# Two passes instead of three in the spatial sum, a closing pass over two tiles, a late gelu, and a bias added at the first evacuation

## The chip, the cores and the metric

The kernel runs on one core of one Trainium2 chip. The metric is the device time of one execution of the program, in microseconds (us), on that core. Medians of several executions are given with their range. An execution counts as slow when it is over 1.5% above the fastest of the same kernel; the executions compared here are fast ones. The profile of a kernel is one execution of it; its "span" (first to last instruction) is some 1.5 to 2 us shorter than the time. The profile also gives the clock that TensorE was granted, as a share of full speed.

Engine names in the profile: PE is TensorE's matmuls, PEld its weight loads, DVE is VectorE, ACT is ScalarE, POOL is GpSimd.

## The reference

Two layers, each an attention block and then a mixer over the sequence, both with residuals. S = 2048 rows, D = 512, 32 heads of 16 that share one key and value head, mixer width 1792.

```python
def _A_ref(x, wq, wk, wv, wo):                 # attention
    q = (x @ wq).reshape(B, S, 32, 16) ...
    k = x @ wk; v = x @ wv
    p = softmax(q k^T * 16 ** -0.5)            # 32 x 2048 x 2048 scores
    return (p v) ... @ wo

def _B_ref(x, w_in, w_sp, b_sp, w_out):        # mixer
    z = gelu(x @ w_in)
    z1 = z[..., :896]
    z2 = layernorm(z[..., 896:])
    g = einsum('ts,bsf->btf', w_sp, z2) + b_sp[None, :, None]   # the "spatial" sum over all 2048 rows s
    return (z1 * g) @ w_out

x = x + _A_ref(layernorm(x), ...)
x = x + _B_ref(layernorm(x), ...)
# and both once more
```

## The kernel before

All data is bf16, with f32 sums in PSUM (the memory that the matmuls write to; an instruction that takes a sum out of it is called an evacuation here). The kernel is written as a generator: a Python list scheduler gives every instruction a priority, dependencies and an estimated duration, and lays out the order of all five engines when the kernel is built. The parts that matter here:

- The softmax needs exp of 4096 score blocks of 128x512 (2048 a layer). ScalarE does most of them, in instructions of 3 or 2 blocks; VectorE does the rest with a polynomial, in six lines of instructions for a batch of 3 blocks.
- Rows are finished in groups ("chunks"). When a chunk's attention is done, its part of the mixer up to z2 is computed beside the softmax of the next chunk. A gelu on ScalarE interrupts the exps and costs two table loads, one there and one back.
- The spatial sum needs z2 of all 16 row tiles of 128. Tiles come with the chunks, so the sum is made in passes: each pass multiplies the tiles that are ready and adds the result into an fp16 buffer `gp`. The last tile is done in a closing pass, which also multiplies by z1 and by w_out.
- Two PSUM banks serve all of these side jobs and VectorE's score blocks.
- "Warm-up" matmuls, zero times zero, are put in where TensorE has had little to do in the last 3.41 us, to keep its clock up.

The passes, the batches of gelu by chunk, and the number of tiles left to the closing pass:

```python
        self.chunks = [[256, 256, 512, 512, 256, 128, 128], [512, 512, 512, 256, 128, 128]]
        self.passes = [[(0, 8, 2), (8, 12, 3), (12, 15, 5)], [(0, 8, 1), (8, 12, 2), (12, 15, 4)]]
        self.gelus = [[(0, 1, 2), (3,), (4, 5), (6,)], [(0, 1), (2,), (3, 4), (5,)]]
        self.s_fin = 15
```

The gelu of a batch of chunks, and what follows it:

```python
        # in mixer(), after the matmuls with w_in ...
        if g.ci != batch[-1]:
            return
        T, z1, z2 = [[x for h in self.held for x in h[i]] for i in range(3)]
        zs = [h[3] for h in self.held]
        self.held = []
        t0 = T[0]
        ...
        def gl2(e):
            return e.activation(z2f[:, t0 * FH:(t0 + nt) * FH], z2f[:, t0 * FH:(t0 + nt) * FH], ACTF.Gelu_apprx_tanh)
        if last:
            gs = z2
            pre = sc.op("act", lambda e: e.activation(self.tiny[:], self.mhalf[:], ACTF.Exp), 0.1, z1 + z2, 2.0, table="exp")
        else:
            gs = [sc.op("act", gl2, d_gelu(nt * FH), z1 + z2, -1.0, table="gelu")] * (2 * nt)
            z1 = [sc.op("act", gl1, sum(d_gelu(NF * zn) for _t, zn, _v in zs), z1 + z2, -0.9, table="gelu")]
        ... # z1 goes to DRAM; z2 is normalized tile by tile (bn_stats, bn_aggr, pow, tensor_scalar)
        sc.rush = 0.0
        for (s0, s1, ci) in self.passes[g.layer]:
            if ci == g.ci:
                self.spatial(s0, s1, g.layer)
        if last:
            self.closing(g.layer)
```

One pass of the spatial sum. The bias is a matmul of its own, the `None` in `seq`; the first pass is copied out of PSUM, later passes are added to `gp`:

```python
    def spatial(self, s0, s1, layer):
        sc = self.sc
        acc = s0 > 0
        nst = s1 - s0
        early = s1 == self.s_fin
        pr = 1.6 if early else 2.5 if acc else 4.0
        ... # where the weight slabs of this pass are loaded to
            for f in range(NF):
                seq = ([] if acc else [None]) + list(range(s0, s1))

                def pe(e, b, part, tc=tc, f=f, w_=w_, seq=seq):
                    ins = None
                    for s in part:
                        st, sp = (s == seq[0]), (s == seq[-1])
                        if s is None:
                            ins = e.matmul(self.b32(b), self.ident[:, tc:tc + 1].to_broadcast([P, P]), self.b4[:, :],
                                           start=st, stop=sp)
                        else:
                            ins = e.matmul(self.b32(b), self.z2n[:, s, f * 128:(f + 1) * 128],
                                           w_[:, s - s0, :] if s - s0 < na or not spare else wsp[:, s - s0 - na, :],
                                           start=st, stop=sp)
                    ...
                def ev_fn(e, b, tc=tc, f=f):
                    dst = self.gp[:, tc, f, :]
                    if acc:
                        return e.tensor_tensor(dst, self.b32(b), dst, ALU.add)
                    return e.tensor_copy(dst, self.b32(b))
                pl, (ev,) = sc.job(pieces, [dict(
                    fn=ev_fn, dur=d_psum(512), prio=max(1.0, pr - 1.5),
                    deps=list(self.gp_read[(tc, f)]) + ([self.gp_ops[(tc, f)]] if acc else []))], deps, pr)
```

VectorE takes no score block while a job of the last ("early") pass is ready and has not started:

```python
    def take(self, t, js):

        k = self.k
        sc = k.sc
        if self.hold or sc.bank_free() > t:
            return None
        base = NDB * (self.nb % (NPD // NDB))
        if any(o.start is None and o.ready is not None and o.ready <= t for o in k.early_first):
            return None
        want = sum(o.first and o.prio < URGENT and o.ready <= t for o in sc.ready["pe"])
```

The rule for warm-up matmuls: one is due when the columns multiplied in the last 3.41 us are fewer than the sum in this line, with TICK_COLS = 3060 and WARM = 1600.

```python
        t = sc.below(f, TICK_COLS + WARM + (AHEAD if near else 0.0))   # WarmStream.peek()
```

The softmax here doesn't subtract the row's maximum and nothing guards it: scores larger than these inputs give would overflow.

Of the kernel before, what the change touches and what calls it, by code (L numbers as in the profile page):

```python
# [13 lines left out]
P = 128  # L14
# [6 lines left out]
NF = 7  # L21
# [352 lines left out]
NDB = 3  # L374

# [7 lines left out]
WARM = 1600.0  # L383
# [46 lines left out]
class Kern:  # L430
    def __init__(self, nc, A_x, A_wq, A_wk, A_wv, A_wo, B_x, B_w_in, B_w_sp, B_b_sp, B_w_out, out):
# [10 lines left out]
        self.passes = [[(0, 8, 2), (8, 12, 3), (12, 15, 5)], [(0, 8, 1), (8, 12, 2), (12, 15, 4)]]  # L442
        self.gelus = [[(0, 1, 2), (3,), (4, 5), (6,)], [(0, 1), (2,), (3, 4), (5,)]]
        self.s_fin = 15
# [17 lines left out]
        self.V = sb([P, self.NT, 128], BF16, "V")  # L462
# [5 lines left out]
        self.b4 = sb([P, 512], BF16, "b4")  # L468
# [95 lines left out]
    def load(self, A_x, A_wq, A_wk, A_wv, A_wo, B_b_sp):  # L564
# [24 lines left out]
        zb = sc.op("pool", lambda e: e.memset(self.b4[:], 0.0), 0.5, (), 4.0)  # L589
        self.l_b = self.dma(lambda e: e.dma_start(self.b4[0:4, :], B_b_sp.rearrange("(k t) -> k t", k=4)), [zb], "ldb", 4096)  # L590
# [39 lines left out]
        m = vm(self.V[:], 2048, 0.13)  # L630
        self.z1s_free = [self.c_wk]
        self.c_v = pm(self.V[:].rearrange("p t (c r) -> p t c r", r=32)[:, :, :, DH], 1.0, 64, 0.8, [m])
# [54 lines left out]
    def layer_keys(self, layer):  # L687
        sc = self.sc
        for p in range(8):
            def build(p=p):  # L690
# [28 lines left out]
                def vcp(b):  # L719
                    return (self.V[:, ts[0]:ts[0] + 2, :].rearrange("p t (c r) -> p t c r", r=32)[:, :, :, 0:DH],  # L720
                            self.b32(b)[:, 256:256 + 2 * DH].rearrange("p (t d) -> p t d", t=2)[:, :, None, :].to_broadcast([P, 2, 4, DH]))
# [5 lines left out]
                vc = dict(fn=lambda e, b: e.tensor_copy(*vcp(b)), dur=d_psum(128), prio=pr, deps=[self.c_v] + vd_,  # L727
                          alts=[("act", lambda e, b: e.activation(*vcp(b), ACTF.Copy), d_act(128) + 0.1)])
# [106 lines left out]
    def finish_group(self, g, pv_last):  # L835
        sc = self.sc
        nq = g.n // 128
        sc.rush = RUSH if g.fin <= 1 and g.v == 1 else 0.0
# [120 lines left out]
    def mixer_chunk(self, g):  # L959
# [5 lines left out]
        pr = PR_LAST if last else (PR_SMALL if g.fin <= 2 else 3.0)  # L965
# [32 lines left out]
        if last:  # L998
            z1v = self.z1L
            z1_war = list(self.dx_s.end)  # L1000
        elif g.ci < batch[-1] <= self.passes[g.layer][0][2]:
            z1v = self.gp[:, g.ci].bitcast(BF16)[:, :, 0:n]
            z1_war = [o for f in range(NF) for o in self.gp_read[(g.ci, f)]]
        else:
            z1v = self.z1s[:].rearrange("p (f t) -> p f t", f=NF)
            z1v = z1v[:, :, 256:256 + n] if g.fin == 1 else z1v[:, :, 0:n]
            z1_war = list(self.z1s_free)
# [27 lines left out]
        if g.ci != batch[-1]:  # L1035
            return
        T, z1, z2 = [[x for h in self.held for x in h[i]] for i in range(3)]
# [12 lines left out]
        def gl2(e):  # L1050
            return e.activation(z2f[:, t0 * FH:(t0 + nt) * FH], z2f[:, t0 * FH:(t0 + nt) * FH], ACTF.Gelu_apprx_tanh)
        if last:
            gs = z2
            pre = sc.op("act", lambda e: e.activation(self.tiny[:], self.mhalf[:], ACTF.Exp), 0.1, z1 + z2, 2.0, table="exp")
        else:
            gs = [sc.op("act", gl2, d_gelu(nt * FH), z1 + z2, -1.0, table="gelu")] * (2 * nt)
            z1 = [sc.op("act", gl1, sum(d_gelu(NF * zn) for _t, zn, _v in zs), z1 + z2, -0.9, table="gelu")]
        for ci, (zt, zn, v) in zip(batch, zs):
            sp = self.dma(lambda e, zt=zt, zn=zn, v=v: e.dma_start(self.z1_dv[:, :, zt * 128:zt * 128 + zn], v), z1,
                          f"z1s{g.layer}{zt}", zn * P * NF * 2)  # L1060
            self.z1_spill.append((zt * 128, zt * 128 + zn, sp))
            if last:
                self.z1L_spill = sp
            elif ci < batch[-1] <= self.passes[g.layer][0][2]:
                for f in range(NF):
                    self.gp_read[(ci, f)] = [sp]
            else:
                self.z1s_free = [sp] + (self.z1s_free if g.fin == 1 else [])
        ag = []
# [15 lines left out]
        sc.rush = 0.0  # L1085
        for (s0, s1, ci) in self.passes[g.layer]:
            if ci == g.ci:
                self.spatial(s0, s1, g.layer)
        if last:
            self.closing(g.layer)  # L1090
# [10 lines left out]
    def spatial(self, s0, s1, layer):  # L1101
# [4 lines left out]
        pr = 1.6 if early else 2.5 if acc else 4.0  # L1106
        z2f = self.z2n[:].rearrange("p t f -> p (t f)")
        wsl = self.wsT[:].rearrange("p s t -> p (s t)")
        if early:

            self.wsP = []
            nf = self.NT - s1
            parts = [(0, 2, z2f[:, 2048:5120], (2, 3, 4, 5)), (2, 3, z2f[:, 5120:6656], (5, 6, 7)),
                     (3, 4, wsl[:, 0:1536], None)]
            for (c0, c1, w_, tiles) in parts:
                w_ = w_.rearrange("p (s t) -> p s t", s=nst)
                war = self.last_ws[0] if tiles is None else [o for t in tiles for o in self.z2_read[t]]
                ld = self.dma(lambda e, w_=w_, c0=c0, c1=c1: e.dma_start(w_, self.ws_dv[:, s0:s1, 512 * c0:512 * c1]),
                              war + self.ws_st[s0:s1], f"wsp{c0}", (c1 - c0) * nst * 131072, 1.0)
                for tc in range(c0, c1):  # L1120
                    self.wsP.append((w_[:, :, 512 * (tc - c0):512 * (tc - c0 + 1)], ld, tiles))
            self.held_f = range(0, 3)
# [7 lines left out]
        for tc in range(4):  # L1130
            if early:
                w_, ld, held = self.wsP[tc]
# [14 lines left out]
            for f in range(NF):  # L1147
                seq = ([] if acc else [None]) + list(range(s0, s1))

                def pe(e, b, part, tc=tc, f=f, w_=w_, seq=seq):  # L1150
                    ins = None
                    for s in part:
                        st, sp = (s == seq[0]), (s == seq[-1])
                        if s is None:
                            ins = e.matmul(self.b32(b), self.ident[:, tc:tc + 1].to_broadcast([P, P]), self.b4[:, :],
                                           start=st, stop=sp)
                        else:
                            ins = e.matmul(self.b32(b), self.z2n[:, s, f * 128:(f + 1) * 128],  # L1158
                                           w_[:, s - s0, :] if s - s0 < na or not spare else wsp[:, s - s0 - na, :],
                                           start=st, stop=sp)  # L1160
# [3 lines left out]
                deps = [ld] + ([ld2] if spare else []) + [self.z2_op[s] for s in range(s0, s1)] + [self.c_id]  # L1164
# [3 lines left out]
                def ev_fn(e, b, tc=tc, f=f):  # L1168
                    dst = self.gp[:, tc, f, :]
                    if acc:  # L1170
                        return e.tensor_tensor(dst, self.b32(b), dst, ALU.add)  # L1171
                    return e.tensor_copy(dst, self.b32(b))
# [222 lines left out]
class ExpStream:  # L1395
# [31 lines left out]
    def commit(self, t):  # L1427
# [18 lines left out]
        if not nx or nx[0].unit.grp.layer != blocks[0].unit.grp.layer:  # L1446
            if not self.queue:
                for x, (b, n) in enumerate(k.rings["full"]):
                    for i in range(b, b + n):
                        k.sc.lend(i, [i], k.fill_s.exp_of[x])  # L1450
                k.sc.op("act", lambda e: e.activation(k.tiny[:], k.mhalf[:], ACTF.Gelu_apprx_tanh), 0.1, [o, k.c_mh], -2.0,
                        table="gelu")


class PVStream:
# [53 lines left out]
    def commit(self, t):  # L1509
# [3 lines left out]
        def fn(e):  # L1513
            ins = None
            for b in u.blocks:
                j = b.j
                ins = e.matmul(k.b32(u.grp.pvb)[32 * j:32 * j + 32, :], k.V[:, u.kt, 32 * j:32 * j + 32], b.slot,  # L1517
# [14 lines left out]
class DexStream:  # L1532
# [29 lines left out]
    def take(self, t, js):  # L1562
# [3 lines left out]
        if self.hold or sc.bank_free() > t:  # L1566
            return None
        base = NDB * (self.nb % (NPD // NDB))
        if any(o.start is None and o.ready is not None and o.ready <= t for o in k.early_first):
# [257 lines left out]
```

## Time and profile before

| | before |
|---|---|
| time, median of 3 (range) | 1803.42 us (1802.94 to 1805.38) |
| span of the profile, mean granted clock | 1800.1 us, 0.999 |
| busy: ACT, DVE, PE | 1725.3, 1699.9, 1604.6 us |
| score blocks on ScalarE / VectorE | 3550 / 546 |
| last exp of layer 0, of layer 1, end | 853.8, 1749.1, 1800.1 us |

The head of the profile page of the kernel before: span, busy time of each engine with its share and the number of instructions, and the shares of engines in the chain of work that ended last.

```profile
span 1800.1 us, 29924 instructions
...
PE 1604.6 (89%) x11861; PEld 480.7 (27%) x11949; DVE 1699.9 (94%) x2576; ACT 1725.3 (96%) x1556; POOL 56.2 (3%) x90
...
ACT 45%; DVE 19%; PE 18%; issue 17%; POOL 1%; DMA 0%; ACTq 0%; POOLq 0%; DVEq 0%
```

Three engines are above 89%, so an average does not tell which of them sets the time. The table by windows does. Its rows are stretches of the softmax's end and of the tail of each layer; the columns are named in the first line, with (x) the number of instructions.

```profile
core 0: us, PE busy (x) PEld busy (x) DVE busy (x) ACT busy (x) POOL busy (x), PEclk, DMA share, GB/s
800.00:854.00 54.00, 49.71 (x360) 15.93 (x362) 41.03 (x69) 53.93 (x48) 1.92 (x4) 1.00 0.25 76
854.00:893.00 39.00, 36.07 (x239) 18.98 (x241) 37.78 (x95) 18.44 (x35) 3.63 (x6) 1.00 0.18 50
1640.00:1749.00 109.00, 101.89 (x736) 32.56 (x747) 84.29 (x140) 108.87 (x95) 2.85 (x6) 1.00 0.22 61
...
1763.00:1800.00 37.00, 34.39 (x176) 16.25 (x178) 32.23 (x84) 13.14 (x30) 0.00 (x0) 1.00 0.46 137
```

Until 854 us and until 1749 us ScalarE is busy for 53.93 of 54 and 108.87 of 109 us: in the softmax, time is ScalarE time. In the tail of layer 0 VectorE is the full engine, 37.78 of 39 us, with PE close behind at 36.07. In the last 37 us PE and VectorE have 34.39 and 32.23 us and take turns.

ScalarE's timeline shows the two places where the change acts: a gelu interruption before the end of layer 0, and the closing pass at the end. Columns: start, duration, engine, line, operation, and in brackets the idle time before it with its releaser.

```profile
829.47 1.28 ACT L1051 ACT_TABLE_LOAD   x1
...
835.65 1.28 ACT L1434 ACT_TABLE_LOAD   x1
836.94 16.84 ACT L1434 ACTIVATE Pa<-ps_all 128x1536 bf16<-128x1536 f32 x15
853.80 1.28 ACT L1451 ACT_TABLE_LOAD   x1
...
1749.07 1.28 ACT L1451 ACT_TABLE_LOAD   x1
...
1770.18 0.60 ACT L1229 ACTIVATE E<-ps_all 128x512 f16<-128x512 f32 x1 [3.52 <-PE ps_all L1217]
...
1778.54 0.60 ACT L1229 ACTIVATE E<-ps_all 128x512 f16<-128x512 f32 x1 [4.01 <-PE ps_all L1217]
```

The interruption takes from 829.47 to 836.94, 7.5 us without an exp, 2.56 of them table loads. The closing repeats every 8.36 us (1770.18, 1778.54), two blocks of 256 columns each time.

The groups of VectorE instructions by form (count, then busy us and mean ns, then idle before them) give the price of an evacuation and of a score block:

```profile
L1626 DVE TENSOR_SCALAR E<-ps_all 128x512 f32<-128x512 f32 x546 | 368.7, 681 | 27.1 <-PE ps_all L1774 25.2
...
L1171 DVE TENSOR_TENSOR gp<-ps_all,gp 128x512 f16<-128x512 f32 x112 | 74.5, 684 | 19.4 <-PE ps_all L1158 19.0
...
L1172 DVE CAST gp<-ps_all 128x512 f16<-128x512 f32 x56 | 38.0, 679 | 1.4 <-PE ps_all L1158 1.2
```

There are 168 evacuations of the spatial sum of 0.68 us each. A batch of three score blocks takes 3 x 0.681 for the first line plus five more lines (1.750, 0.950, 0.949, 0.949 and 0.549 us), 2.4 us a block. What ScalarE's exps waited for scores, from the list of waits (total us, times, longest):

```profile
ACT Pa L1434 <- PE ps_all L1774: 11.7, 20, 1.0
```

### The profile page before, as it was taken

How to read it: one execution, taken by the hardware profiler on the slowest of the kernel's cores; microseconds unless marked ns; L12 is line 12 of the kernel's file. 1: busy time of each engine (PE TensorE's matmuls, PEld its weight loads, DVE VectorE, ACT ScalarE, POOL GpSimd, SP SyncE). 2: the span in 40 equal slices, each digit the busy share in tenths (PEclk: the TensorE clock that was granted, in tenths of full speed). 3: DMA queues.
4: the chain of work that ended last, by engine and by line, in shares of the span. 5: the costliest groups of instructions: out<-in, count | busy, mean ns of one | idle time of the engine just before them, and what ended most of it. 6: DMA issues, size and time to landing. Idle time of an engine off the chain costs nothing.

```text
span 1800.1 us, 29924 instructions
## 1 busy us (share of the span) xinstructions
PE 1604.6 (89%) x11861; PEld 480.7 (27%) x11949; DVE 1699.9 (94%) x2576; ACT 1725.3 (96%) x1556; POOL 56.2 (3%) x90
## 2 busy tenths in 40 slices
PE   8888888888989999999998888888889899998999
PEld 4222222222222222223432222222222222222234
DVE  9999999999999999987999999999999889999868
ACT  8999999999999999999589999999999999999993
POOL 2000000000000000000110000000000000000000
PEclk9999999999999999999999999999999999999999
DMA  5444100011011011222120000000111111202223
GB/s 159 100 89 120 58 14 7 7 31 21 16 44 31 27 24 36 60 68 66 53 45 7 7 7 18 18 7 4 30 22 15 45 30 30 50 28 52 64 57 113
DMA packets 155427, 75.64 MB, mean 42 GB/s; under 512 B 108564, under 2 KB 151704, under 8 KB 155288
## 3 DMA queue, kind: packets, MB, share of 16 engines
q1 hardware_dynamic: 153704, 73.56, 15.9%
q8 instruction: 95, 1.56, 0.4%
q10 hardware_dynamic: 1584, 0.16, 0.1%
q14 instruction: 44, 0.36, 0.1%
HBM read 30.97 MB, written 17.83 MB: 27 GB/s over the span
## 4 chain that ended last, share of the span: by engine, by line
ACT 45%; DVE 19%; PE 18%; issue 17%; POOL 1%; DMA 0%; ACTq 0%; POOLq 0%; DVEq 0%
ACT Pa L1434 43%; PE ps_all L1774 5%; PE ps_all L1517 3%; DVE E L1626 3%; PE ps_all L1158 3%; DVE Pd L1657 3%; PE ps_all L1250 2%; PE ps_all L1755 2%; DVE E L1653 1%; DVE E L1655 1%; DVE E L1651 1%; DVE st L641 1%; DVE st L1071 1%; PE ps_all L980 1%; DVE gp L1171 1%
## 5 line engine op out<-in xcount | busy, mean ns | idle before, releaser
L1434 ACT ACTIVATE Pa<-ps_all 128x1536 bf16<-128x1536 f32 (+1 forms) x1425 | 1612.7, 1391 | 13.7 <-PE ps_all L1774 11.7
L1774 PE MATMUL ps_all<-qs,kT 32*128 32x512 bf16 x4096 | 560.1, 385 | 154.1 <-ACT Pa L1434 140.1
L1626 DVE TENSOR_SCALAR E<-ps_all 128x512 f32<-128x512 f32 x546 | 368.7, 681 | 27.1 <-PE ps_all L1774 25.2
L1755 PE MATMUL ps_all<-zero 128*128 128x512 bf16 x1241 | 374.3, 386 | 13.4 <-DVE st L1071 3.7
L1774 PEld LDWEIGHTS ps_all<-qs,kT 32*128 32x128 bf16 x4096 | 138.8, 91 | 728.1 <-ACT Pa L1434 693.5
L1517 PE MATMUL ps_all<-Pa,V 128*32 128x512 bf16 x3550 | 322.1, 385 | 0.9 <-DVE oT L841 0.9
L1657 DVE SCALAR_TENSOR_TENSOR Pd<-E 128x1536 uint16<-128x1536 f32 (+2 forms) x185 | 319.0, 1724 | 2.3
L1158 PE MATMUL ps_all<-wsT,z2n 128*128 128x512 bf16 x668 | 188.4, 382 | 8.7 <-issue 3.9
L1517 PE MATMUL ps_all<-Pd,V 128*32 128x512 bf16 x546 | 187.0, 386 | 0.0
L1655 DVE TENSOR_TENSOR E<-E 128x1536 f16<-128x1536 f16 (+2 forms) x185 | 173.3, 937 | 2.0
L1653 DVE TENSOR_TENSOR E<-E 128x1536 f16<-128x1536 f16 (+2 forms) x185 | 173.2, 936 | 2.0
L1651 DVE TENSOR_SCALAR E<-E 128x1536 f16<-128x1536 uint16 (+2 forms) x185 | 173.1, 936 | 1.4
L1755 PEld LDWEIGHTS ps_all<-zero 128*128 128x128 bf16 x1241 | 92.1, 97 | 203.6 <-issue 145.2
L1654 DVE TENSOR_SCALAR E<-E 128x1536 f16<-128x1536 f16 (+2 forms) x185 | 100.4, 543 | 0.8
L1517 PEld LDWEIGHTS ps_all<-Pa,V 128*32 128x32 bf16 x3550 | 64.7, 94 | 120.9 <-issue 113.6
L1171 DVE TENSOR_TENSOR gp<-ps_all,gp 128x512 f16<-128x512 f32 x112 | 74.5, 684 | 19.4 <-PE ps_all L1158 19.0
L1158 PEld LDWEIGHTS ps_all<-wsT,z2n 128*128 128x128 bf16 x714 | 56.6, 98 | 88.5 <-issue 43.6
L980 PE MATMUL ps_all<-w_in_r,xnTB 128*128 128x448 bf16 x256 | 64.2, 355 | 2.0 <-DVE z2n L991 1.0
L1016 PE MATMUL ps_all<-xnTB,w_in_r 128*128 128x512 bf16 (+2 forms) x364 | 63.0, 299 | 1.1 <-DVE z1s L1027 0.6
L1250 PE MATMUL ps_all<-E 128*128 128x512 bf16 x214 | 52.2, 380 | 4.1 <-DVE E L1235 2.6
L645 POOL TENSOR_SCALAR ve<-mv 128x2 f32<-128x2 f32 (+1 forms) x28 | 11.9, 423 | 1358.4 <-DVE mv L643 1358.3
L841 DVE CAST oT<-ps_all 128x512 bf16<-128x512 f32 x64 | 43.6, 682 | 4.5 <-PE ps_all L1517 4.4
(87 smaller groups left out, 919.0 us busy)
## 6 DMA issues: line engine op xcount, KB each, us to landing
wsT_scratch<-gp SPq DMA_DIRECT2D x16, 512.0 KB, 3.7
wsT<-wsT_scratch SPq DMA_DIRECT2D x8, 1024.0 KB, 5.3
z1s<-z_scratch SPq DMA_DIRECT2D x16, 448.0 KB, 3.7
wsT<-wsT_scratch SPq DMA_DIRECT2D x8, 512.0 KB, 3.5
z_scratch<-z1s SPq DMA_DIRECT2D x4, 896.0 KB, 5.2
X<-in_A_x_dram SPq DMA_DIRECT2D x8, 256.0 KB, 5.5
out_dram<-X SPq DMA_DIRECT2D x16, 128.0 KB, 1.9
w_in_r<-in_B_w_in_dram SPq DMA_DIRECT2D x1, 1792.0 KB, 10.2
```

The source lines that it names most:

```text
L1158: ins = e.matmul(self.b32(b), self.z2n[:, s, f * 128:(f + 1) * 128], w_[:, s - s0, :] if s - s0 < na or not spare else wsp[:, s - s0 - na, :],
L1171: return e.tensor_tensor(dst, self.b32(b), dst, ALU.add)
L1434: return e.activation(k.Pa[:, base:base + n, :], k.b32(b0, n).rearrange("p (k q) -> p k q", k=n), ACTF.Exp, scale=SCALE)
L1517: ins = e.matmul(k.b32(u.grp.pvb)[32 * j:32 * j + 32, :], k.V[:, u.kt, 32 * j:32 * j + 32], b.slot, tile_position=(0, 32 * j), start=u.fir ...
L1626: c = k.sc.op("dve", lambda e: e.tensor_scalar(k.ey[:, s, 512 * i:512 * (i + 1)], k.b32(j.bank.idx)[:, 0:512], E_LOG2, E_BIAS, op0=ALU.mul ...
L1651: o2 = sc.op("dve", lambda e: e.tensor_scalar(x, lo, E_X * 2.0 ** -16, E_X * E_A, op0=ALU.mult, op1=ALU.add), d_sb(n, 0.521e-3), self.ops ...
L1653: o3 = sc.op("dve", lambda e: e.tensor_tensor(w, x, x, ALU.mult), d_sb(n, 0.521e-3), [o2, self.wfree], pr)
L1654: o4 = sc.op("dve", lambda e: e.tensor_scalar(w, w, E_C, None, op0=ALU.add), d_sb(n, 0.26e-3), [o3], pr)
L1655: o5 = sc.op("dve", lambda e: e.tensor_tensor(w, w, x, ALU.mult), d_sb(n, 0.521e-3), [o4], pr)
L1657: o7 = sc.op("dve", lambda e: e.scalar_tensor_tensor(po.bitcast(U16), y, E_D, w, op0=ALU.add, op1=ALU.add), d_sb(n, 1.042e-3), [o5] + self ...
L1755: return e.matmul(k.b32(pvb if b is None else b.idx), k.zero[:], k.zero[:, None, :].to_broadcast([P, 4, P]), start=b is not None, stop=b i ...
L1774: return e.matmul(self.b32(bank), self.kT[32 * j:32 * j + 32, g.v, kt * 128:(kt + 1) * 128], self.qs[32 * j:32 * j + 32, g.q.slot, :], til ...
```

## The change

The intent is to take work off VectorE (the spatial sum's evacuations fall from 168 to 112) and off ScalarE (one gelu interruption fewer inside each layer's softmax), at the price of a longer closing. Its core:

```diff
-WARM = 1600.0
+WARM = 1200.0
...
-        self.passes = [[(0, 8, 2), (8, 12, 3), (12, 15, 5)], [(0, 8, 1), (8, 12, 2), (12, 15, 4)]]
-        self.gelus = [[(0, 1, 2), (3,), (4, 5), (6,)], [(0, 1), (2,), (3, 4), (5,)]]
-        self.s_fin = 15
+        self.passes = [[(0, 8, 2), (8, 14, 4)], [(0, 8, 1), (8, 14, 3)]]
+        self.gelus = [[(0, 1, 2), (3, 4), (5,), (6,)], [(0, 1), (2, 3), (4,), (5,)]]
+        self.s_fin = 14
...
-        self.V = sb([P, self.NT, 128], BF16, "V")
+        self.V = sb([P, self.NT, 32], BF16, "V")
-        self.b4 = sb([P, 512], BF16, "b4")
+        self.bb = sb([P, S], BF16, "bb")                 # b_sp on all 128 partitions, 512 KB written by one DMA
...
+        if g.fin == 1 and not self.exps_done:            # the last but one chunk: gelu after the last exp
+            sc.rush = 0.0
+            self.late = (g, last, pr, batch)
+            return
+        self.mix_rest(g, last, pr, batch)
...                                                        # in spatial()
-                seq = ([] if acc else [None]) + list(range(s0, s1))
+                seq = list(range(s0, s1))
-                    if acc:
-                        return e.tensor_tensor(dst, self.b32(b), dst, ALU.add)
-                    return e.tensor_copy(dst, self.b32(b))
+                    return e.tensor_tensor(dst, self.b32(b), dst if acc else self.bb[:, 512 * tc:512 * tc + 512], ALU.add)
...                                                        # after the last exp of a layer
+                k.exps_done = True
+                if k.late is not None:
+                    k.mix_rest(*k.late)
+                    k.late = None
```

Cut: V is kept once instead of four times (this pays for `bb` in SBUF), the late batch's gelu and second norm are split by chunk, priorities of the passes, a bound on how far ahead VectorE takes score blocks, and the addresses of the weight slabs.

By the instruction order: 56 bias matmuls fewer, spatial matmuls of 512 columns 840 to 784, closing matmuls of 256 columns 112 to 224, evacuations 168 to 112, warm-up matmuls 1241 to 1111, table loads 17 to 13, score blocks on VectorE 546 to 540.

## The prediction

> **What bounds the kernel now.** The table by windows shows ACT busy 99 to 100 us of nearly every 100 during softmax; its 75 us of idle lie at the start (8), where layer 0 ends (840 to 960: 29) and at the end (1740 to 1800: 32). The chain of waits gives 43% to ACT's exp line. In the timeline a pair of exps (3 + 2 blocks of 128x512) repeats every 2.26 us: 0.4525 us a block. DVE computes 546 of the 4096 blocks at 2.395 us each (its six exp lines, 1308 us). So softmax time is ACT time: 3550 blocks, table loads (1.283 us each), gelus. The tails are bound otherwise: after layer 0 DVE (39.4 of 40 us at 880 to 920), PE close behind; at the end a latency chain from last exp (1749.1) to closing matmuls (1762.7), then PE and DVE alternate for 34 us, 8.36 us per two column blocks (7.56 of matmuls, 0.216 us for 512 columns, 0.108 for 256).
>
> **What the change does, by the instruction order.**
> - 56 bias matmuls and 56 evacuations fewer (168 to 112, 0.68 us each: -38 us of DVE). DVE could take 16 more blocks for it, but takes 540 blocks, six fewer: the second pass (tiles 8 to 13) fills the last two groups of each layer, where no exp block goes to DVE. ACT gets +2.7 us; freed DVE time becomes idle.
> - ACT inside the softmax: one gelu interruption fewer per layer: -2 table loads (2.57 us) and one tile's gelu (2 x 0.93) moved behind the last exp: -8.9 us in both layers. Copies move to ACT: +1.1. With the blocks about -5 us, all on the critical path.
> - Closing over two tiles: +56 matmuls of 256 columns per layer, +6 us of PE each.
> - Tail of layer 0: 12 evacuations fewer behind the last exp (-7 us DVE), one tile's second norm more (+1.9); PE -3.2 + 6. Net -1 us.
> - Tail of layer 1: 46 instead of 31 spatial matmuls between last PV and closing (+3.2 us PE, about half hidden); the closing becomes PE-bound, 9.1 instead of 8.36 us per two blocks (+3). The late gelu fits ACT's 1.76 us gap. Sum +5 us.
> - V evacuation 128 to 32 columns, larger b_sp load, 130 fewer warm-up matmuls: within 1 us.
>
> Sum about -2 us; shorter ACT waits on PE (11.7 us in all) may add.
>
> **Predicted: 1800 us, range 1790 to 1808 (8 in 10).** Faster by over 2%: 0.02; within 2%: 0.95; slower by over 2%: 0.03.
>
> **What would show each step.** Right: exp busy on ACT up 3 us, table loads 17 to 13; last exp of layer 1 4 to 7 us earlier; DVE busy about 50 us lower and idle in the last 55 us of each softmax; last exp to end about 56 us instead of 51. Wrong: last exp no earlier, or final tail no longer.
>
> **What would make it wrong.** (a) Fewer warm-up matmuls (threshold 1600 to 1200): the Trainium skill, page "TensorE: Matmul & The Clock Gate", section "What's actually happening", says the array runs at half clock after an idle window of about 3.4 us; before was granted 0.999 on average, so its trace hardly tests it. Dips: above 1808. (b) PE may limit the second pass (168 matmuls, 36 us, beside 152 exp blocks, 69 us). (c) The layer 0 tail may be more DVE-bound than I think: down to 1790.

## The result

A ratio here is the mean time of one kernel's fast runs over that of the other's of the same rounds, so it is not quite the ratio of the medians that are quoted.

| | before | after |
|---|---|---|
| median (range), 6 runs each | 1803.18 us (1801.05 to 1806.33) | 1803.24 us (1802.57 to 1807.56) |
| ratio (95%) | | 1.0004 (0.9989 to 1.0019): same |
| profile: span, granted clock | 1800.1 us, 0.999 | 1801.9 us, 0.995 |

The time did not move. But the profile after is not the profile before: four stages moved, two each way. The third column is a second profile of the same kernel, taken later as a control. The mark that separates tail and softmax is the start of the first exp after the first 54 score blocks that ScalarE does in layer 1; "last exp" is the start of the table load right after it.

| stage, us | before | after | after, again | predicted shift |
|---|---|---|---|---|
| start to last exp of layer 0 | 853.8 | 850.4 (-3.4) | 849.3 (-4.5) | -2.6 |
| tail of layer 0, to the mark | 79.2 | 77.6 (-1.6) | 77.8 (-1.3) | -1 |
| mark to last exp of layer 1 | 816.1 | 818.5 (+2.4) | 818.1 (+2.0) | -2.6 |
| last exp of layer 1 to end | 51.0 | 55.4 (+4.4) | 55.4 (+4.4) | +5 |
| span | 1800.1 | 1801.9 (+1.8) | 1800.6 (+0.5) | -1.2 |

The last column is worked out from the prediction's own terms: 8.9 us of gelus and tables less 1.1 of copies and 2.7 of six blocks make 5.1 us, put down half to each layer here; its own sum was rounded to -2. (By the traces four of the six blocks fall in layer 0, where VectorE's went from 277 to 273, so the terms are rather -2.1 and -3.0.)

The head of the page of the kernel after:

```profile
span 1801.9 us, 29641 instructions
...
PE 1583.2 (88%) x11819; PEld 471.6 (26%) x11819; DVE 1653.8 (92%) x2489; ACT 1725.2 (96%) x1558; POOL 54.1 (3%) x99
```

VectorE lost 46 us of work (1699.9 to 1653.8), PE 21, and ScalarE next to nothing. The windows of the same four stages:

```profile
800.00:850.00 50.00, 49.95 (x360) 15.71 (x359) 16.79 (x29) 49.63 (x44) 0.81 (x2) 1.00 0.16 51
850.00:887.00 37.00, 36.35 (x261) 20.15 (x260) 33.15 (x87) 20.24 (x37) 4.31 (x8) 1.00 0.28 76
1640.00:1746.00 106.00, 99.28 (x687) 30.59 (x687) 64.56 (x108) 104.49 (x89) 3.96 (x8) 0.98 0.15 43
...
1762.00:1802.00 40.00, 38.82 (x234) 22.09 (x232) 33.54 (x85) 14.59 (x29) 0.00 (x0) 1.00 0.42 125
```

VectorE now has 16.79 us of work in the last 50 us of layer 0's softmax, and 64.56 in the last 106 of layer 1's: freed and not used. PE is full in the first of these stretches (49.95 of 50), with the second pass, as the prediction's point (b) feared; ScalarE lost little by it (49.63 of 50 busy). The columns are those of the table before. In the last 106 us of layer 1's softmax ScalarE is idle for 1.5 us (104.49 busy), where before had 0.13 of 109, and the granted clock there is 0.98, where the stretches of before had 1.00.

ScalarE's timeline at the interruption, behind the last exp of layer 0, and in the closing:

```profile
762.88 4.90 ACT L1458 ACTIVATE Pa<-ps_all 128x1024 bf16<-128x1024 f32 x4
767.80 1.28 ACT L1071 ACT_TABLE_LOAD   x1
769.09 4.78 ACT L1071 ACTIVATE z2n<-z2n 128x3584 bf16<-128x3584 bf16 x2
...
850.38 1.28 ACT L1475 ACT_TABLE_LOAD   x1
...
851.91 0.95 ACT L1071 ACTIVATE z2n<-z2n 128x896 bf16<-128x896 bf16 x1
852.77 0.93 ACT L1067 ACTIVATE z1s<-z1s 128x896 bf16<-128x896 bf16 x1
...
1772.13 1.69 ACT L1253 ACTIVATE E<-ps_all 128x512 f16<-128x512 f32 x3 [2.86 <-PE ps_all L1241]
...
1781.24 1.69 ACT L1253 ACTIVATE E<-ps_all 128x512 f16<-128x512 f32 x3 [2.86 <-PE ps_all L1241]
```

The late chunk's gelu is now behind the last exp (850.38 to 853.70) where ScalarE has nothing else; before, it interrupted the exps. From the end of the last exp before the gelu at 767.78 (762.88 + 4.90) to the start of the gelu at 769.09 there are 1.31 us, nearly all of it the table load of 1.28. The Trainium skill, page "ScalarE: Activation LUTs", section "What ACT_TABLE_LOAD costs", gives 1283 ns for the load, which the trace confirms, and another 1380 ns of drain, which is not to be seen here. The closing repeats every 9.11 us (1772.13, 1781.24), as against 8.36 before.

The VectorE groups that answer to those of before, by form:

```profile
L1654 DVE TENSOR_SCALAR E<-ps_all 128x512 f32<-128x512 f32 x540 | 363.9, 682 | 24.4 <-PE ps_all L1802 21.6
...
L1196 DVE TENSOR_TENSOR gp<-ps_all,gp 128x512 f16<-128x512 f32 x56 | 38.5, 688 | 50.2 <-PE ps_all L1184 50.1
L1196 DVE TENSOR_TENSOR gp<-ps_all,bb 128x512 f16<-128x512 f32 x56 | 38.3, 683 | 0.8 <-PE ps_all L1184 0.4
```

Evacuations fell from 168 to 112 at the same price, and the bias comes in at no cost: 683 ns with `bb` against 679 for the plain copy. The 56 adds of the second pass were preceded by 50.1 us of idle waiting for PE, so VectorE is not what holds that pass. And the waits of ScalarE's exps for scores:

```profile
ACT Pa L1458 <- PE ps_all L1802: 17.4, 30, 1.5
```

17.4 us in 30 waits, as against 11.7 in 20. In layer 1 from the mark on, ScalarE's busy time fell from 814.7 to 812.6 us (-2.1, and 812.8 in the control), but its idle time rose from 1.4 to 5.9 us (5.3 in the control). So the expected gain of layer 1 was there, and a new wait took it back.

3.8 us of layer 1's waits lie beside stretches where the granted clock dipped: near 952, 1399 to 1404, and 1649 us. But a dip is not the whole of it. From the mark on, the exps of the control wait 4.6 us for scores, those of before 0.55 us. Only 2.0 of the 4.6 us lie beside a dip (near 952 and 1335 us). The other 2.6 us are six waits where its clock was full (0.55 at 931 us, 0.29 at 1122, 0.45 and 0.46 at 1400 to 1402, 0.39 at 1571, 0.44 at 1699), and all but one are found in the first profile too, at nearly the same times and within 0.01 us of the same size; the one at 1402 is hidden there in a longer wait beside a dip. So about half of the new waits belong to this order of the instructions, whatever the clock does.

The profile of before has one dip of the clock, that of after has five, that of the control two. All are at half clock, 3.4 us long, or 6.8 for one of the control. One dip of the control, microsecond by microsecond (the table by windows):

```profile
944.00:945.00 1.00, 0.96 (x12) 0.19 (x10) 1.00 (x1) 1.00 (x2) 0.00 (x0) 1.00 0.00 0
945.00:946.00 1.00, 0.39 (x2) 0.09 (x2) 0.72 (x1) 1.00 (x2) 0.00 (x0) 1.00 0.00 0
946.00:947.00 1.00, 0.59 (x10) 0.21 (x10) 0.00 (x0) 1.00 (x3) 0.00 (x0) 1.00 0.00 0
947.00:948.00 1.00, 1.00 (x12) 0.21 (x4) 0.02 (x1) 1.00 (x3) 0.00 (x0) 0.68 0.02 8
948.00:949.00 1.00, 1.00 (x5) 0.16 (x4) 0.68 (x1) 1.00 (x2) 0.00 (x0) 0.50 0.00 0
949.00:954.00 5.00, 5.00 (x27) 0.90 (x24) 4.41 (x6) 4.04 (x5) 0.00 (x0) 0.50 0.00 0
954.00:955.00 1.00, 1.00 (x14) 0.23 (x14) 0.94 (x2) 0.54 (x2) 0.00 (x0) 0.90 0.00 0
```

The columns are again those of the first table by windows; the granted clock is third from the right. PE is busy for 0.96, 0.39 and 0.59 us of three microseconds, so it is idle for 1.06 of 3 us, and then the clock falls to 0.68 and 0.50 for about 7 us, while PE has no idle time at all. PE gets through 27 matmuls in the 5 us from 949, where the microseconds at 944 and 954 have 12 and 14. ScalarE is busy for 4.04 of these 5 us.

The same profile has a stretch in which PE had still less to do, and no dip came of it:

```profile
1398.00:1399.00 1.00, 0.33 (x8) 0.00 (x0) 1.00 (x4) 1.00 (x2) 0.00 (x0) 1.00 0.00 0
1399.00:1400.00 1.00, 0.39 (x3) 0.13 (x3) 1.00 (x3) 0.59 (x1) 0.00 (x0) 1.00 0.00 0
1400.00:1401.00 1.00, 0.66 (x4) 0.31 (x4) 1.00 (x3) 0.95 (x1) 0.00 (x0) 1.00 0.00 0
```

PE is busy for 1.38 of these 3 us, the clock stays at 1.00, and ScalarE waits for scores all the same (0.59 busy in the second microsecond). So in this trace the busy time of three microseconds does not by itself decide whether a dip follows.

How much is a lower clock worth? Over fast runs of both kernels, clock and span go together:

| | runs | mean clock | mean span | slope per 0.001 of clock | fitted span at clock 0.996 |
|---|---|---|---|---|---|
| before | 33 | 0.9965 | 1802.4 us | -1.00 us (r = -0.95) | 1802.9 us |
| after | 12 | 0.9934 | 1803.0 us | -0.96 us (r = -0.86) | 1800.5 us |

So after is about 2.4 us shorter at the same clock (standard error 0.6), and runs at a clock lower by 0.0031, worth about 3 us by this slope. One dip of 3.4 us at half clock lowers the mean of 1800 us by 0.0009, so by this slope it goes with about 1 us of time. The fit is an estimate, and what it shows is that the two go together: the slope may also hold what goes along with a dip, such as the gap that brought it on.

### The profile page after: what moved, and what is told of

It reads as the page before. It is cut to its first block, busy times and chain, and to the rows that moved or that the text cites. A ratio compares the mean times of both kernels' runs of the same rounds, so it can differ in the third digit from the quotient of the medians.

```text
span 1801.9 us, 29641 instructions
## 1 busy us (share of the span) xinstructions
PE 1583.2 (88%) x11819; PEld 471.6 (26%) x11819; DVE 1653.8 (92%) x2489; ACT 1725.2 (96%) x1558; POOL 54.1 (3%) x99
## 4 chain that ended last, share of the span: by engine, by line
ACT 41%; PE 25%; DVE 18%; issue 15%; DMA 1%; POOL 0%; ACTq 0%
ACT Pa L1458 41%; PE ps_all L1184 7%; PE ps_all L1802 7%; PE ps_all L1545 4%; DVE E L1654 3%; DVE Pd L1685 2%; PE ps_all L1274 2%; DVE E L1679 1%; DVE st L1112 1%; DVE E L1683 1%; DVE E L1681 1%; DVE st L648 1%; PE ps_all L1783 1%; PE ps_all L986 1%; PE ps_all L1025 1%
## 5 line engine op out<-in xcount | busy, mean ns | idle before, releaser
L1458 ACT ACTIVATE Pa<-ps_all 128x1536 bf16<-128x1536 f32 (+1 forms) x1426 | 1615.2, 1399 | 19.1 <-PE ps_all L1802 17.4
L1783 PE MATMUL ps_all<-zero 128*128 128x512 bf16 x1111 | 342.6, 391 | 15.3 <-DVE st L1112 5.3
L1685 DVE SCALAR_TENSOR_TENSOR Pd<-E 128x1536 uint16<-128x1536 f32 x180 | 314.8, 1749 | 2.3
L1681 DVE TENSOR_TENSOR E<-E 128x1536 f16<-128x1536 f16 x180 | 171.0, 950 | 2.5
L1683 DVE TENSOR_TENSOR E<-E 128x1536 f16<-128x1536 f16 x180 | 171.0, 950 | 1.9
L1679 DVE TENSOR_SCALAR E<-E 128x1536 f16<-128x1536 uint16 x180 | 171.1, 951 | 1.3
L1184 PE MATMUL ps_all<-wsT,z2n 128*128 128x512 bf16 x616 | 168.9, 384 | 1.9 <-DVE gp L1196 0.9
L1783 PEld LDWEIGHTS ps_all<-zero 128*128 128x128 bf16 x1111 | 83.0, 98 | 191.5 <-issue 132.8
L1682 DVE TENSOR_SCALAR E<-E 128x1536 f16<-128x1536 f16 x180 | 98.9, 550 | 0.8
L1196 DVE TENSOR_TENSOR gp<-ps_all,gp 128x512 f16<-128x512 f32 x56 | 38.5, 688 | 50.2 <-PE ps_all L1184 50.1
L1184 PEld LDWEIGHTS ps_all<-wsT,z2n 128*128 128x128 bf16 x616 | 45.7, 98 | 77.2 <-issue 37.5
L652 POOL TENSOR_SCALAR ve<-mv 128x2 f32<-128x2 f32 (+1 forms) x28 | 10.6, 379 | 1412.2 <-DVE mv L650 1412.1
L1253 ACT ACTIVATE E<-ps_all 128x512 f16<-128x512 f32 (+1 forms) x51 | 26.1, 540 | 25.4 <-PE ps_all L1241 24.7
```

Of the source, the lines that this page charges most:

```text
L1458: return e.activation(k.Pa[:, base:base + n, :], k.b32(b0, n).rearrange("p (k q) -> p k q", k=n), ACTF.Exp, scale=SCALE)
L1679: o2 = sc.op("dve", lambda e: e.tensor_scalar(x, lo, E_X * 2.0 ** -16, E_X * E_A, op0=ALU.mult, op1=ALU.add), d_sb(n, 0.521e-3), self.ops ...
L1681: o3 = sc.op("dve", lambda e: e.tensor_tensor(w, x, x, ALU.mult), d_sb(n, 0.521e-3), [o2, self.wfree], pr)
L1682: o4 = sc.op("dve", lambda e: e.tensor_scalar(w, w, E_C, None, op0=ALU.add), d_sb(n, 0.26e-3), [o3], pr)
L1683: o5 = sc.op("dve", lambda e: e.tensor_tensor(w, w, x, ALU.mult), d_sb(n, 0.521e-3), [o4], pr)
L1685: o7 = sc.op("dve", lambda e: e.scalar_tensor_tensor(po.bitcast(U16), y, E_D, w, op0=ALU.add, op1=ALU.add), d_sb(n, 1.042e-3), [o5] + self ...
```

## The experiments

The theory: the time is ScalarE's and TensorE's; VectorE's freed time is not used and not needed; the late gelu is worth some 7 us; the closing gives back about 5; and the rest is lost to a lower clock, because 130 warm-up matmuls are missing. The rivals: VectorE's freed time is already used somewhere (then giving the work back costs as much as it freed); or the gain was there to be had and only the rule that keeps score blocks off VectorE wastes it; or the clock is not a matter of how many warm-up matmuls there are, but of how the order of the instructions fell out.

Twelve kernels ran, four to a call, each call with 11 runs of the kernel before on the same chip. Those medians were 1804.49, 1803.64 and 1804.32 us. Every kernel gave correct results but for one, which is told with it. A kernel is compared with the changed kernel through its ratio to the kernel before; the changed kernel's own is 1.0004, and 1.0007 in the repeat (0.9994 to 1.0020). A difference of 1 to 3 us from the changed kernel is inside these intervals and is not told apart from noise. No run tested the two passes, the new priorities or the bound on how far ahead VectorE takes score blocks on their own.

### The changed kernel again (after_again)

No edit.

> The changed kernel itself, as a control on this chip and for the spread of its granted clock. Both theories: 1802 to 1807 us; run by run the time follows the mean granted clock, about 1 us for each 0.001, from 0.991 to 0.995, as in its six earlier runs.

Measured: 1805.95 us (1802.43 to 1808.33, 6 runs), ratio 1.0007 (0.9994 to 1.0020). The result repeats, stage by stage too (the table above). One term of one stage differs between the profiles by up to 1.1 us, and that is the precision of what follows.

### VectorE work given back in the second pass (dup2)

```diff
                     dst = self.gp[:, tc, f, :]
+                    if acc:
+                        e.bn_stats(self.junk[:, (tc * NF + f) % 8, :], self.b32(b))
                     return e.tensor_tensor(...)
```

56 extra instructions of 0.695 us on VectorE, which read the bank and write to scratch: 38.9 us of work, as much as the change took off.

> The changed kernel with one more VectorE instruction of about 0.6 us (statistics of the same PSUM bank, result unused) at each of the 56 evacuations of the second spatial pass: +34 us of VectorE where its trace shows it idle, instruction order otherwise the same. Theory (VectorE time saved there is worth nothing): 1803 to 1807 us, the few us from the evacuations that fall behind the last exp. Rival (the saved evacuations did buy time, and something else took it back): 1815 us or more.

Measured: 1810.07 us (1808.74 to 1813.75, 6 runs), ratio 1.0035 (1.0021 to 1.0049). That is 0.0028 to 0.0031 above the changed kernel, 5 to 6 us for 38.9 us of work. The last exps of the layers come at 851.9 and 1751.0 us, against 850.4 and 1746.5, and the last tail took 57.3 us instead of 55.4. So about 85% of the freed work was indeed not on the critical path. The time is above the 1803 to 1807 us of the theory and well below the 1815 us of the rival. In the profile, 2.1 and 1.9 of the 6.4 us are in the two tails, where a few of these evacuations still lie.

### The same work in the first pass (dup1)

```diff
                     dst = self.gp[:, tc, f, :]
+                    if not acc:
+                        e.bn_stats(self.junk[:, (tc * NF + f) % 8, :], self.b32(b))
                     return e.tensor_tensor(...)
```

> The same 56 extra VectorE instructions, but at the evacuations of the first spatial pass, where VectorE is about 96 percent busy with exp chains. Theory (place decides): ScalarE begins to wait, 1810 to 1830 us, clearly above the run with the same extra work in the second pass. Rival (VectorE is nowhere decisive): the same time as that run, within 2 us.

Measured: 1837.19 us (1833.57 to 1839.70, 4 runs), ratio 1.0179 (1.0164 to 1.0195). The same 38.7 us of VectorE work, 31 us of time. The table by windows for 500 to 760 us, where layer 0's first pass lies, first of the run with the work in the first pass and then of the one with it in the second:

```profile
500.00:760.00 260.00, 224.27 (x1661) 60.60 (x1659) 249.32 (x351) 246.27 (x217) 1.87 (x4) 0.99 0.14 37
```

```profile
500.00:760.00 260.00, 236.62 (x1776) 63.80 (x1774) 250.37 (x348) 259.98 (x232) 2.80 (x6) 1.00 0.15 40
```

ScalarE is busy for 246.27 us instead of 259.98: it lost 13.7 us. Both have VectorE at about 250 of 260, so VectorE has no room there for the added work. The list of waits of ScalarE's exps for scores over the whole run, in the same order:

```profile
ACT Pa L1461 <- PE ps_all L1805: 42.9, 81, 1.6
```

```profile
ACT Pa L1461 <- PE ps_all L1805: 19.4, 34, 1.3
```

And the list of waits of PE: how long score matmuls (this line) waited for VectorE's evacuations into `gp`, same order:

```profile
PE ps_all L1805 <- DVE gp L1199: 13.9, 18, 1.8
```

```profile
PE ps_all L1805 <- DVE gp L1199: 0.2, 1, 0.2
```

An extra 0.69 us where VectorE is already full delays the release of the bank, then the scores (13.9 us instead of 0.2), then the exps (42.9 instead of 19.4). This shows both halves of the theory: added VectorE work is dear beside the first pass, and close to free beside the second, which is where the change saved it. Two caveats: the extra instruction also holds the PSUM bank for 0.7 us more, and this run does not tell the two apart; and its mean clock was 0.9898 against 0.9937 of the run with the work in the second pass, which by the fit goes with some 4 of the 27 us between the two.

### Score blocks on VectorE also during the second pass (ef0)

```diff
-EF = 1
+EF = 0        # no longer keeps score blocks away while a job of the last pass is ready
```

> The changed kernel without the rule that keeps score blocks away from VectorE while the second pass has a job ready (EF = 0). The order shows 551 blocks on VectorE instead of 540, the extra ones all in the last two or three groups of a layer. Theory (the rule alone wastes the freed VectorE time): ScalarE's exps shrink by 11 x 0.45 = 5 us, time 1797 to 1800 us. Rival (TensorE is full there, 49.95 of 50 us, and the second pass is pushed behind the last exp by as much): last exp 2.5 us earlier in each layer but tails longer, 1802 to 1806 us.

Measured: 1808.65 us (1807.04 to 1811.71, 5 runs), ratio 1.0025 (1.0012 to 1.0039). VectorE took 551 blocks instead of 540, ScalarE's exps fell from 1615.2 to 1611.6 us, and yet the last exps came at 851.0 and 1751.3 us, no sooner. The waits for scores rose to 21.5 us in 35, and both tails got longer (80.7 and 57.5 us). Letting score blocks in did not turn the idle VectorE time into time saved, so the rule did not waste it. Why is argued and not shown: the blocks use the two side banks and the PE time that the second pass needs. The time is above the range of the rival too (1802 to 1806 us).

### More warm-up matmuls, in the same order (w_more)

```diff
         def fn(e):
-            return e.matmul(bank, zero, zero, ...)
+            for _ in range(2 if n % 3 == 0 else 1):
+                ins = e.matmul(bank, zero, zero, ...)
+            return ins
```

371 extra ones; the order of everything else stays as it is.

> The changed kernel with every third warm-up matmul issued twice (371 more, about 80 us of TensorE), order otherwise the same, so that only the activity of TensorE differs. Theory (the lower warm-up threshold lets the clock dip, five dips against one, and ScalarE waits for scores 5 us longer): no dips, ScalarE's wait for score matmuls in all down from 17.4 to about 12 us, 1797 to 1801 us. Rival (the longer waits come from a full TensorE beside the second pass): waits unchanged or longer, 1803 to 1808 us.

Measured: 1810.74 us (1809.53 to 1811.01, 5 runs), ratio 1.0032 (1.0020 to 1.0044). The mean clock rose from 0.9934 to 0.9960, but the dips did not all go (near 159, 773, 951 and 1405 us), the waits for scores stayed (18.3 us in 37), and the time rose by about 5 us (0.0025 to 0.0028 of 1804). The theory that missing warm-up matmuls cost time fails in this form: in this run more of them went with a higher clock, and cost more than it brought.

### WARM as it was (warm1600)

```diff
-WARM = 1200.0
+WARM = 1600.0
```

> The changed kernel with the old warm-up threshold (1600). Theory (the lower threshold costs granted clock, 0.9938 against 0.9962 in the mean, about 1 us per 0.001): mean clock 0.996 or more, and 1799 to 1802 us. Rival (the clock follows the arrangement of the work, not the threshold; or the rearranged order costs as much, 539 blocks on VectorE): clock unchanged or time 1803 us or more.

Measured: 1806.92 us (1805.82 to 1808.42, 5 runs), ratio 1.0017 (1.0005 to 1.0029). 1295 warm-up matmuls, clock 0.9962: the clock is what it was before, the time is not. But the scheduler also laid out another order (539 blocks on VectorE, the last exp of layer 0 at 853.8 us), so this is not the changed kernel with a better clock. Its exps waited 18.7 us for scores at a clock of 0.997 in the profile, more than the changed kernel's 17.4 at 0.995: long waits do not need a low clock. Its result was wrong, by a hair: a relative error of 0.0200013 where 0.02 is allowed. VectorE's exp is a polynomial, so which blocks go there can change the result.

### Extra warm-up matmuls only where PE has slack (w_gap)

```diff
+        for o, more in self.warms:                      # after the order is laid out
+            if after.get(id(o), o.end) - o.end > 0.22:  # PE's next instruction starts over 0.22 us later
+                more[0] = 2
```

179 of the 1111 are doubled.

> The changed kernel, order unchanged, with a second warm-up matmul only behind those 179 of 1111 after which the schedule leaves TensorE more than 0.22 us free, so that nothing should be delayed. Theory (at equal clock the change is worth 2 to 3 us, and its lower clock takes them back): mean clock 0.996 or more and 1800 to 1802 us, below both kernels. Rival (more warm-up work always delays score matmuls, as it did when every third was doubled): clock up, time 1804 us or more.

Measured: 1808.03 us (1804.73 to 1809.55, 6 runs), ratio 1.0019 (1.0006 to 1.0032), clock 0.9940, waits for scores 18.7 us. The clock gained 0.0006, no more than the kernel before differs (0.9963 to 0.9969), and the time is 2 to 3 us longer, which the intervals do not tell from none. No gain shows. Whether the scheduler's slack was there on the chip was not looked at.

### The kernel before, with fewer warm-up matmuls (b_thin)

```diff
         def fn(e):
+            if n % 9 == 0:
+                return e.matmul(bank[:, 0:64], zero, zero[:, 0:64], ...)
             return e.matmul(bank, zero, zero, ...)
```

138 of 1241 cut from 512 to 64 columns, which is about what the change takes out, in the old order.

> The kernel before, order unchanged, with every ninth warm-up matmul cut from 512 to 64 columns (138 of 1241 all but gone, as many as the change dropped). Theory (the warm-up matmuls hold the clock, and the clock sets the spread): mean clock below the 0.9966 of the kernel before, near 0.994, and about 2 to 3 us longer, 1805 to 1807 us. Rival (these few make no difference): clock 0.996 to 0.997 and the time of the kernel before within 1 us.

Measured: 1802.44 us (1800.51 to 1805.96, 6 runs), ratio 0.9994 (0.9979 to 1.0008), clock 0.9958, waits 10.6 us. The expected slowdown did not come. The clock fell by 0.0007, a quarter at most of what separates after from before. A fit to these six runs gives 1800.6 us at a clock of 0.996, 2.3 us less than before. So taking these warm-up matmuls out of the old order cost nothing that shows, and their number explains a part of the changed kernel's lower clock at most.

### The late gelu taken back (nolate)

```diff
-        if g.fin == 1 and not self.exps_done:
+        if False:
...
-            if g.fin == 1:
+            if g.fin == 1 and self.exps_done:
```

> The changed kernel with the gelu of the last chunk but one back inside the softmax (no waiting for the last exp). Theory (an interruption costs its table loads and its gelu on ScalarE): +2.57 +1.87 us per layer inside the softmax, less what the tail gains, so 1808 to 1813 us, table loads 17 instead of 13. Rival (late gelu only moves work into a tail that is critical as well): within 2 us of the control.

Measured: 1811.44 us (1809.94 to 1815.76, 6 runs), ratio 1.0045 (1.0031 to 1.0059), 7 us more than the changed kernel (0.0038 x 1804 us). The last exps come at 857.9 and 1755.9 us, 8.6 and 10.7 us later than in the control; the last tail is 53.8 us, 1.6 shorter. There are 21 table loads, not the 17 that I counted on: an exp slipped between the two gelus of the batch, which are separate instructions now, so each layer has two interruptions. So the 7 us hold a second interruption a layer that the late gelu is not to be credited with: four table loads of 1.28 us, 5.1 us on ScalarE. Where ScalarE's time is the kernel's time, that leaves some 2 us (an estimate), or 4 by the two profiles, which are 9.1 us apart, for a kernel that keeps its gelus together. The run shows that an interruption costs time in the softmax; the 2 to 4 us were not measured.

### The bias alone (biasonly)

The kernel before, with `bb` added at the first evacuation, V kept once, and no bias matmuls:

```diff
-                seq = ([] if acc else [None]) + list(range(s0, s1))
+                seq = list(range(s0, s1))
-                    if acc:
-                        return e.tensor_tensor(dst, self.b32(b), dst, ALU.add)
-                    return e.tensor_copy(dst, self.b32(b))
+                    return e.tensor_tensor(dst, self.b32(b), dst if acc else self.bb[:, 512 * tc:512 * tc + 512], ALU.add)
```

> The kernel before with the bias part alone: b_sp added at the first evacuation instead of 56 matmuls, and V kept once instead of four times (which pays for the memory). Theory (TensorE leads nowhere inside the softmax): no gain, within 2 us of the kernel before apart from the rearranged order. Rival (the bias matmuls cost their 12 us of TensorE): 1795 us or less.

Measured: 1806.03 us (1802.43 to 1810.24, 6 runs), ratio 1.0009 (0.9994 to 1.0025). No gain, as the theory has it: 56 matmuls of 0.216 us are 12 us of PE time that did not show in the time. The order was another one (547 blocks on VectorE, 1275 warm-up matmuls), so a gain of a few us could be hidden.

### The closing over two tiles alone (close2)

The kernel before with its third pass over tiles 12 and 13, and the closing over 14 and 15; the slab addresses follow.

```diff
-        self.passes = [[(0, 8, 2), (8, 12, 3), (12, 15, 5)], [(0, 8, 1), (8, 12, 2), (12, 15, 4)]]
-        self.s_fin = 15
+        self.passes = [[(0, 8, 2), (8, 12, 3), (12, 14, 5)], [(0, 8, 1), (8, 12, 2), (12, 14, 4)]]
+        self.s_fin = 14
```

> The kernel before with one part of the change alone: its third pass sums tiles 12 and 13, and tiles 14 and 15 are left to the closing pass (two tiles instead of one). Theory: the closing after layer 1 becomes bound by TensorE, from its first to its last 256-column matmul 3 to 4 us longer than the kernel before (8.36 us per two column blocks become about 9.1); in all 1804 to 1809 us. Rival (TensorE's extra 6 us hide behind VectorE): the closing keeps its length.

Measured: 1813.16 us (1805.80 to 1818.05, 6 runs), ratio 1.0048 (1.0027 to 1.0070). From the first closing matmul to the end took 40.6 us as against 37.4 before, +3.2, and the last tail 54.6 as against 51.0, +3.6: the size that the theory gave for the closing. The rest of the 9 us is not the closing: the runs spread widely, at a mean clock of 0.9915, and the profiled run, at 0.998, had a span of 1804.0, only 3.9 above before. 555 blocks went to VectorE, so the order was another one again.

### The threshold a little higher (warm1300)

```diff
-WARM = 1200.0
+WARM = 1300.0
```

> The changed kernel with a warm-up threshold of 1300 instead of 1200; its order gives VectorE 546 blocks as in the kernel before, so ScalarE has 6 fewer than the changed kernel. Theory (ScalarE's blocks and the clock decide): -2.7 us for the blocks and a clock a little higher, 1799 to 1802 us. Rival (a rearranged order costs more than that, as with 1600): 1804 us or more.

Measured: 1797.81 us (1797.63 to 1798.10, 5 runs), ratio 0.9965 (0.9953 to 0.9978): 6 us faster than before, and the only kernel that is clear of the noise below both. It is still within 2%. 546 blocks go to VectorE (not 540), there are 1154 warm-up matmuls, the mean clock is 0.9986, and its profile has one dip (near 1675 us), as that of before. Its stages against before: last exp of layer 0 at 848.7 us (-5.2), tail 79.6 (+0.4), layer 1's softmax 811.8 (-4.3), last tail 56.0 (+5.0). With no loss of blocks, the prediction's terms are -3.9 for each layer's softmax (8.9 less 1.1 of copies, halved), -1 and +5. So this order has what the change was to bring in the softmaxes; its exps waited 14.2 us for scores, less than the changed kernel's 17.4. It does not show that 1300 is a better threshold: 1600, with a clock nearly as good as before, gave 1806.9.

## Why the prediction was right

The time was right, 1800 us (1790 to 1808) against 1803.24, and so was "within 2%". Part of that is luck. The range is 18 us wide and holds the time of no change at all, and the change of -2 us that was forecast was not seen (+0.06 us). Layer 0's softmax gained 0.8 to 1.9 us more than forecast, which made up for some of what layer 1's missed, 4.6 to 5.0 us. Point by point:

1. **VectorE's freed time becomes idle.** Predicted about -50 us of VectorE and no gain; measured -46, and idle beside the second pass. Shown by the run with the work given back there (5 to 6 us of time for 38.9 us of work), by the same work in the first pass (31 us, some 4 of them with a lower clock), and by letting score blocks in (no gain).
2. **Exps on ScalarE up by 3 us, table loads 17 to 13.** Measured 1612.7 to 1615.2 us (+2.5), and 13 loads. Right.
3. **Gelus and tables, about -5 us with the blocks.** ScalarE's busy time in layer 1 fell by 2.1 us, and layer 0's last exp came 3.4 to 4.5 us sooner, where 2.6 a layer was predicted. The run without the late gelu took some 7 us more, 5.1 us of table loads for a second interruption included. Right as a mechanism; the size of the late gelu alone was not measured.
4. **Tail of layer 0, -1 us.** Measured -1.3 to -1.6.
5. **Last tail, +5 us, with 9.1 us for two column blocks.** Measured +4.4, and 9.11. The closing over two tiles alone gave +3.6 in the same tail.
6. **Last exp of layer 1 4 to 7 us earlier.** Wrong: 2.6 and, in the control, 3.9. The step that failed is the hope that "shorter ACT waits on PE (11.7 us in all) may add". The waits for scores grew, to 17.4 us (15.5), and of the 5.1 us that were to come from the softmaxes, layer 1 gave back 2.0 to 2.4 instead of bringing 2.6. About half of the new waits stand beside dips of the clock, the other half at fixed places with the clock full, which the prediction had no term for. "V evacuation 128 to 32 columns, larger b_sp load, 130 fewer warm-up matmuls: within 1 us" left no room for a lower clock either. The prediction saw that danger under its point (a), and expected dips to show as a time above 1808 or not at all. The runs showed a term in between: a mean clock lower by 0.0031, which by the fit goes with about 3 us. By the same fit, the change is worth -2.4 us at equal clock, close to the forecast -2; that is an estimate, and no run held the clock.

The reason given for the lower clock, the missing warm-up matmuls, is at most a small part of it. 371 more gave +0.0026 of clock, 179 more +0.0006, and 138 cut in the kernel before gave -0.0007: the signs agree, but 130 matmuls cover at most about a third of 0.0031. And in no run that kept the order did adding them gain time. What is left is how the order fell out: the clock was 0.9934 and 0.9986 for two layouts of the same change. Which gap brings on a dip, and why, is left open. The Trainium skill, page "TensorE: Matmul & The Clock Gate", section "What's actually happening", tells of an idle window of about 3.4 us; here the clock fell after three microseconds in which PE was busy for 1.94 us in all, so in this trace a stretch busy for two thirds was no protection, while another, busy for 1.38 of 3 us, went without a dip. The same page, in "A second HAM failure mode: psum-queue depth-cycling", tells of short idle times between groups of matmuls that let the clock swing, which is closer to what is seen, though the three profiles above have only one to five dips each.

## What to carry to other kernels

Work taken off an engine counts only where that engine ends the wait: the same 39 us of VectorE work cost 31 us beside the first pass and 5 to 6 us beside the second. When a change cancels out, cut the run into stages and ask of each stage whether the busy time or the idle time of its limiting engine moved; here, in layer 1, the busy time fell and new waits took it back. In a kernel whose order comes from a scheduler, a parameter moves hundreds of instructions, so test a suspected cost in a frozen order as well, and try neighbouring settings before judging the change: the spread between the layouts for thresholds of 1200, 1300 and 1600 (9 us) is larger than the effect of the change.

## What the Trainium skill lacked or had wrong

- Page "TensorE: Matmul & The Clock Gate", section "What's actually happening": it names an idle window of about 3.4 us as what lowers the clock. Here the clock fell to 0.50 after three microseconds with PE busy for 0.96, 0.39 and 0.59 us, 1.06 us of idle in all, and stayed there for about 7 us while PE was fully busy. In the same profile PE was busy for 0.33, 0.39 and 0.66 us of three microseconds, and the clock stayed at 1.00.
- The same section calls the ramp less than 1% of a typical kernel. That agrees: the spans of one kernel, from 1799.5 to 1805.2 us, differ by 0.3%. What it lacks is that the spread from run to run can go with the clock: about 1 us per 0.001 of mean granted clock here (r = -0.95 over 33 runs).
- The pages that I read give no price for filler matmuls that keep the clock up: 371 more of 1111 went with a mean clock higher by 0.0026 and cost about 5 us of 1804.
- Page "ScalarE: Activation LUTs", section "What ACT_TABLE_LOAD costs": it counts a drain of about 1.38 us with each switch, 2.66 us in all. Here a switch between exp and gelu took 1.31 us from the end of one to the start of the other, 1.28 of them the load.
